# Layer 1's last couple in seven factor products, and layer 2's weights prepared in two thirds of the steps

## The chip, the core and the metric

The kernel runs on one core of a Trainium2 chip. TensorE (PE) multiplies 128x128 weight tiles with a moving tile of up to 512 columns into PSUM banks; VectorE (DVE) and ScalarE (ACT) do the elementwise work, each strictly in the order in which its instructions were issued; GpSimd (POOL) does one small operation per attention tile; SyncE (SP) issues the DMAs, also in order. The metric is the device time of one execution in microseconds. A difference of 0.2% (3.1 us) is about what a measurement can tell from no change.

## The reference

```python
kv = einsum('bhsd,bhse->bhde', k, v);  out = einsum('bhsd,bhde->bhse', q, kv)      # linear attention
x = out / sqrt(mean(out*out, -1) + 1e-6) * g_norm                                   # per head of 64
x = x.transpose(0, 2, 1, 3).reshape(4608, 512)
h = x @ w_in1;  x = (h * sigmoid(1.702 * h)) @ w_out1                               # layer 1, d_ff 2048
h = x @ w_in2;  r = maximum(h, 0);  y = (s * r * r + b) @ w_out2                    # layer 2
```

All in float32. The weights come as float64 words and are turned into float32 on the chip; every product is made of three matmuls on a high and a low part of its operands.

## The kernel before, in words

The 4608 tokens are nine blocks of 512. **Head.** The first 48 steps (FIRST to `N1`, here S0 to S47) compute layer 1 for blocks 0, 1 and 2, one step for one 128-row slice f of the hidden layer: 12 matmuls into one `h` bank (`mm1`), Gelu on ACT (`act_g`), a split into high and low parts, 12 matmuls of the second product (`mm2`) two steps later. Blocks 0 and 1 run first, S32 to S47 are block 2 alone, with a single `h` bank (`h0`). Beside them, layer 1's weights are converted (`to_f32`), split and stored, the sums of its first product's factors are prepared (`prep_first`), and attention tiles are computed.

**Pairs.** What is left is computed in couples of two blocks, by a scheme that needs 7 block products where plain blocking needs 8. Layer 1 has three couples (blocks 3 to 8), layer 2 four couples and one single block. A couple is worked off in 8 pairs of slices, a pair in 7 ticks; a tick is one `product` of 6 matmuls (of the first product, `x @ w_in`), what `after` does with it, and one unit of the second product. I count ticks from the first pair: couple 1 is T0 to T55, couple 2 T56 to T111, couple 3 T112 to T167, layer 2 from T168.

Second product, before: in layer 1 every pair has 8 `units` of 6 matmuls each, 4 into a passing bank (name `z`), whose result DVE adds to a sum in SBUF, and 4 into banks that stay (`sum`). The passing bank is `h1` alone up to pair 12 and alternates between `h1` and `a1` from pair 13 (`FREE_A`); `a1` serves the attention tiles meanwhile. With one bank the next z unit cannot begin before DVE's addition of the last is done. In layer 2 the second product too is made in seven factor products: two pairs form a quad, which has 14 `quad_unit`s of 6 matmuls (name `m` for a passing, `msum` for a staying bank), preceded by additions (`factor_add`) and splits (`factor_hi`, `factor_lo`) on ACT and DVE, and followed by `combine` at the couple's end. The quads use `wraw0`, `wraw1`, `wst0`, `wst1` for their raw tiles, the same places that the preparation of layer 2's weights uses.

**Beside the pairs.** Attention tiles for the coming couple are placed by hand (`tiles_in`): in pairs 1, 2, 4, 5 and 9 to 12, at tick 0 and tick 3 of the pair `att_u` (PE), `att_sq` (ACT) and `att_r` (DVE, `ms<-xn`, then POOL), two ticks later `att_norm` (DVE, `xn<-u,r`), and after the product of the third tick `att_turn` (PE, `xtp<-ident,xn`). Everything else is a `Task`, stepped in `background` at a tick's end when its due time has come or the metered load of ACT and DVE is below a limit. Two tasks prepare layer 2's weights: `convert2` (float64 words to float32, 32 slices, 2 ACT and 5 DVE operations each) and `prepare2` (sums `wc`, splits through staging tiles `wst`, stores). Before, they start at about T6 and their due times run to T165.

Of the kernel before, what the change touches and what calls it, by code (L numbers as in the profile page):

```python
# [44 lines left out]
ROOM = 500.0  # L45

# [6 lines left out]
def tile_attn_moe_moe2(  # L53
# [101 lines left out]
    def to_f32(which, ph, f):  # L155
# [5 lines left out]
        w = rot("wf", 3, (P, DM), U32)  # L161
# [58 lines left out]
    def spaced():  # L220
        while couples_on and now[0] < stored[0] + 2:
            yield 1
        stored[0] = now[0]

    def parts_hl(dst, src, n):

        yield
        yield from spaced()
        t = rot("wst", 2, (P, 2, 2, KP), F32R)[:, 0:n]
# [3 lines left out]
        if isinstance(dst, list):  # L233
            for x, part in enumerate(dst):
                move(part, t[:, x])
        else:
            move(dst, t)
# [29 lines left out]

    wt_dram = {}

    def prep_out(p):  # L270

        wa, wb = (w_raw.pop((1, 1, f)) for f in (2 * p, 2 * p + 1))
        if p == 0:
            wt_dram.update({x: dp.tile([P, 8, 2, 2, KP], F32, name=f"wt{x}") for x in range(KF // 4)})
        a, b = (x.rearrange("p (h e) -> p h e", h=2) for x in (wa, wb))
        d = wt_dram[p // 2][:, :, p % 2]
        c = new("wc", (P, 4, KP))
        tt = vector.tensor_tensor
# [235 lines left out]
    def fac_sums(s):  # L514
# [10 lines left out]
        if s > first2:  # L525
# [7 lines left out]
    def split_x(s, i):  # L533

        lay, m, _ = couples[s]
        if i == 6 and s > first2:
# [18 lines left out]
    made2 = [0, 0]  # L555

    def convert2():

        for m, (which, f) in enumerate(order2):
            made2[0] = m  # L560
            while m >= made2[1] + 3:
                yield 1
            for n, _ in enumerate(to_f32(which, 1, f)):
                yield 1 if n == 0 else 0
            if m + 2 < len(order2):
                load_w(order2[m + 2][0], 1, order2[m + 2][1])
        made2[0] = len(order2)

    def prepare2():

        for m, (which, f) in enumerate(order2):
# [4 lines left out]
            yield from (prep_in, prep_out)[which](f // 2)  # L576
            made2[1] = m + 1
# [69 lines left out]
    P2 = first2 * (KF // 2)  # L647
    place_of = {}
# [53 lines left out]

    def width(P_):
# [3 lines left out]
    def c_new(P_, e):  # L707

        if layer(P_):
            q_, m = (P_ - P2) // 2, width(P_)  # L710
# [33 lines left out]
    def g_hi(P_, e):  # L744

        if layer(P_):
            return
# [12 lines left out]
    def g_lo(P_, e):  # L760
        if layer(P_):
# [46 lines left out]
    def units(P_):  # L808
# [48 lines left out]
    FREE_A = 13  # L857
    BY = 2
    FACTORS = 7
# [3 lines left out]
    quads = [(s_, x) for s_ in range(first2, LAST) for x in range(KF // 2 // BY)]  # L863
    t_t, f_t, mid_t, m_ps, m_sb = {}, {}, {}, {}, {}
    t_next = [0]

    def load_t():
# [3 lines left out]
        if n < len(quads) * FACTORS:  # L871
            q_, k_ = divmod(n, FACTORS)
            t = t_t[q_, k_] = new(f"wo{n % T_RING}", (P, 2, 2, KP), F32R)
            move(t, wt_dram[quads[q_][1]][:, k_])
        elif n < len(quads) * FACTORS + KF - 2:
            load_last(n - len(quads) * FACTORS, f"wo{n % T_RING}")

    def load_last(f, tag):
        t = t_t["last", f] = new(tag, (P, 2, 2, KP), F32R)
        move(t, wt_dram[f // 4][:, (slice(0, 8, 7), slice(5, 7))[f % 2], f // 2 % 2])  # L880
# [130 lines left out]
    def combine(s):  # L1011
# [4 lines left out]
        def send(k_, t, right, h):  # L1016
            row, col = js[t] * BT, (2 * right + h) * P
            turns["z"] = turns.get("z", -1) + 1
            z = new(("tr0", "kv0", "kv1")[turns["z"] % 3] if last else ("tr0", "ev0", "g1")[turns["z"] % 3], name="turned")
# [63 lines left out]
    def load_wo2():  # L1083
# [4 lines left out]
        if n < first2 * KF:  # L1088
# [86 lines left out]
    for x, slot in ((0, 2), (0, 2), (0, 5), (0, 5), (1, 5)):  # L1175
        at((P2 + x, slot), "load", load_t)
# [35 lines left out]
    for p in range(KF // 2):  # L1212
        todo.setdefault(10 + 4 * p, []).append((prep_first, p))
# [9 lines left out]
    for m in range(2):  # L1223
        at(len(steps) - 3 + m, "raw", load_w, 0, 1, m)
# [16 lines left out]
    def plan():  # L1241
# [3 lines left out]
        for s_ in range(len(couples)):  # L1245
            n0 = n * s_
            need = []
            if s_:
                if couples[s_][0]:
                    need = [Task(y_get(s_), n0 - n + 6, n0 - n + 7)]  # L1250
                if s_ < LAST:
                    need = [Task(fac_sums(s_), n0 - (14 if s_ <= first2 else 35), n0 - 9, need)]
            for i in range(7 if s_ < LAST else 2):
                if (s_, i) in split_early:
                    continue
                more = [split[s_, 1]] if (i == 6 and s_ <= first2 and (s_, 1) in split) else []
                split[s_, i] = Task(split_x(s_, i), max(0, n0 - 7 + i + 1), max(0, n0 + i - (4 if i < 6 else 5)), need + more)
            if first2 <= s_ < LAST:
# [17 lines left out]
    with tc.manual_schedule():  # L1276
# [204 lines left out]

        split_early = [(0, i) for i in range(4)]
# [6 lines left out]
        for n in range(FIRST, N1):  # L1489
            conv = to_f32(*convs.pop(n)) if n in convs else iter(())  # L1490
            start(n)
            run(n, "splith")
# [9 lines left out]
            run(n, "pe")  # L1502
            next(conv, None)
# [7 lines left out]
            next(conv, None)  # L1511
            y_out(n - 2, 2)
# [7 lines left out]
            make()  # L1520
            make()
            make()
            if n == N1 - 5:
                load_half(0)
# [38 lines left out]
        for P_, (s_, p) in enumerate(pairs):  # L1563
            lay, m, js = couples[s_]
            for i in range(7):
# [4 lines left out]
                at_q = ((P_ - P2) // BY, 7 * (P_ % BY) + i)  # L1570
                after(P_, i)
                if lay:
# [16 lines left out]
                elif i == 2 and layer(P_ - 1) == 0:  # L1589
                    running.append(units(P_ - 1))  # L1590
                for _ in range({6: 2}.get(i, 1) if P_ < P2 else 1 if P_ == P2 or i % 2 == 0 else 0):
# [3 lines left out]
                if lay:  # L1595
# [3 lines left out]
                background(tick, slot, SLACK, ROOM if lay and P_ > P2 + 1 else 9999.0)  # L1599
# [87 lines left out]
```

## Time and profile before

| | |
|---|---|
| three runs | 1569.70, 1569.93 (median), 1570.78 us |
| profiled execution | 1572.51 us, its span 1570.7 us |
| PE busy | 1550.3 us, 99% of the span |
| DVE, ACT busy | 1021.4 us (65%), 936.1 us (60%) |
| DMA | 372.56 MB, mean 237 GB/s |

The columns of the rows further below: a line of the timeline has the start from the span's begin, the duration, engine, line, operation, output and inputs by the program's names, shapes, count, and in brackets the idle time of the engine before it and what ended it. Matmuls of 512 columns show 0.39 us each but start 0.23 us apart: they overlap, so PE's pace is read from the starts. The page and the views name DVE's and ACT's work by one line (L89), that of a helper.

### The profile page before, as it was taken

To read this page: it belongs to the slowest core of one execution; us is meant where nothing else is said; L and a number is where in the kernel's file an instruction comes from. 1 tells how busy PE (TensorE), PEld (TensorE's weight loads), DVE (VectorE), ACT (ScalarE), POOL (GpSimd) and SP (SyncE) were. 2 spreads that over 40 slices of the span, in tenths; PEclk is the share of its full clock that TensorE was granted. 3 is DMA by queue.
4 is the path that set the end of the run, shared out by engine and by line. 5 is a ranking of instruction groups with operands and counts; after the bars stand their busy time and mean duration, and the time that the engine had idled before them with its cause. 6 is when DMAs were issued, how large, how long until landed. Compare 5 with 4: busy or idle time off the path is not lost.

```text
span 1570.7 us, 20568 instructions
## 1 busy us (share of the span) xinstructions
PE 1550.3 (99%) x7536; PEld 1272.0 (81%) x7536; DVE 1021.4 (65%) x1510; ACT 936.1 (60%) x1520; POOL 69.3 (4%) x49
## 2 busy tenths in 40 slices
PE   8999999999999999999999999999999999999999
PEld 7788887878887788888888888788878887888887
DVE  6877733357567666786877366877687768756631
ACT  4766643455455545465445876876687667766652
POOL 3000111201000011000000000000000000000000
PEclk9999999999999999999999999999999999999999
DMA  8679878557876976679885856587568756876574
GB/s 278 192 259 317 287 238 271 202 200 242 276 235 213 319 242 224 229 280 372 330 314 191 285 193 190 191 245 246 188 200 234 238 192 201 224 231 195 189 215 121
DMA packets 185910, 372.56 MB, mean 237 GB/s; under 512 B 79698, under 2 KB 88146, under 8 KB 178642
## 3 DMA queue, kind: packets, MB, share of 16 engines
q1 hardware_dynamic: 185666, 371.12, 71.8%
q8 instruction: 60, 0.98, 0.3%
q14 instruction: 40, 0.33, 0.1%
q10 hardware_dynamic: 144, 0.13, 0.0%
HBM read 289.41 MB, written 81.79 MB: 236 GB/s over the span
## 4 chain that ended last, share of the span: by engine, by line
PE 89%; DVE 5%; ACT 3%; DMA 2%; issue 1%; SPq 0%; POOL 0%; ACTq 0%; DVEq 0%; POOLq 0%
PE A L696 6%; PE A L697 6%; PE A L698 6%; PE m L994 4%; PE m L993 4%; PE m L992 4%; PE D L696 3%; PE D L697 3%; PE D L698 3%; PE z L830 3%; PE sum L830 3%; PE sum L832 3%; PE sum L831 3%; PE z L832 3%; PE z L831 3%; PE acc L624 3%
## 5 line engine op out<-in xcount | busy, mean ns | idle before, releaser
L89 ACT ACTIVATE gh<-gh 128x512 f32<-128x512 f32 x72 | 45.4, 632 | 145.0 <-DVE gh L89 144.8
L994 PE MATMUL m<-fac,wo 128*128 128x512 f32 x320 | 125.2, 391 | 1.1 <-DVE fac L89 1.1
L992 PE MATMUL m<-fac,wo 128*128 128x512 f32 x320 | 125.8, 393 | 0.0
L993 PE MATMUL m<-fac,wo 128*128 128x512 f32 x320 | 125.7, 393 | 0.0
L696 PE MATMUL A<-wi,xl 128*128 128x512 f32 x296 | 116.7, 394 | 1.9 <-ACT wst L89 0.7
L698 PE MATMUL A<-wi,xl 128*128 128x512 f32 x296 | 115.3, 390 | 0.0
L697 PE MATMUL A<-wi,xl 128*128 128x512 f32 x296 | 115.3, 389 | 0.0
L89 DVE TENSOR_TENSOR madd<-m,madd 128x512 f32<-128x512 f32 x122 | 83.8, 687 | 45.8 <-PE m L994 45.7
L89 ACT ACTIVATE wraw<-wraw 128x512 uint32<-128x512 uint32 (+1 forms) x128 | 82.8, 647 | 48.9 <-DVE wraw L89 48.3
L425 POOL TENSOR_TENSOR r<-ms,mhalf 128x8 f32<-128x8 f32 x36 | 65.6, 1825 | 545.7 <-DVE ms L89 545.6
L89 DVE TENSOR_TENSOR fac<-s,fac 128x1024 fp32r<-128x1024 f32 x64 | 77.9, 1218 | 5.5 <-ACT fac L89 5.4
L89 ACT ACTIVATE g<-h 128x512 f32<-128x512 f32 x52 | 31.0, 597 | 79.7 <-PE h L598 70.1
L596 PE MATMUL h<-xh,wi 128*128 128x512 f32 x192 | 76.5, 398 | 1.2 <-ACT g L89 1.2
L830 PE MATMUL z<-wo,wo 128*128 128x512 f32 x192 | 76.1, 396 | 1.2 <-DVE g L89 0.7
L624 PE MATMUL acc<-gh,wo 128*128 128x512 f32 x192 | 76.7, 399 | 0.0
L625 PE MATMUL acc<-gh,wo 128*128 128x512 f32 x192 | 75.0, 391 | 0.8 <-DVE wo L89 0.8
L626 PE MATMUL acc<-gl,wo 128*128 128x512 f32 x192 | 74.9, 390 | 0.0
L598 PE MATMUL h<-xl,wi 128*128 128x512 f32 x192 | 74.9, 390 | 0.0
L832 PE MATMUL z<-wo,wo 128*128 128x512 f32 x192 | 74.8, 390 | 0.0
L831 PE MATMUL z<-wo,wo 128*128 128x512 f32 x192 | 74.8, 389 | 0.0
L597 PE MATMUL h<-xh,wi 128*128 128x512 f32 x192 | 74.8, 389 | 0.0
L994 PEld LDWEIGHTS m<-fac,wo 128*128 128x128 f32 x320 | 59.9, 187 | 16.2 <-DVE fac L89 2.3
(265 smaller groups left out, 4221.4 us busy)
## 6 DMA issues: line engine op xcount, KB each, us to landing
wo<-wt SPq DMA_DIRECT2D x127, 512.0 KB, 4.0
wo<-wo SPq DMA_DIRECT2D x80, 512.0 KB, 5.1
xl<-wi SPq DMA_DIRECT2D x37, 1024.0 KB, 6.4
xl<-wi SPq DMA_DIRECT2D x37, 768.0 KB, 5.6
wi<-wst SPq DMA_DIRECT2D x40, 512.0 KB, 4.4
xh<-wi SPq DMA_DIRECT2D x19, 1024.0 KB, 6.4
wraw<-in_w_in SPq DMA_DIRECT2D x32, 512.0 KB, 4.1
wraw<-in_w_out SPq DMA_DIRECT2D x32, 512.0 KB, 4.7
```

What stands on the lines that cost most here:

```text
L89: return fn(*args, **kw)
L596: nc.tensor.matmul(o, wh[:, cs], xh[:, c, :], start=(c == 0), stop=False)
L624: nc.tensor.matmul(o, wh[:, ds_], gh, start=(f == lo), stop=False)
L696: nc.tensor.matmul(o, wh, xh, start=(c == 0 and not more), stop=False, skip_group_check=more)
L697: nc.tensor.matmul(o, wl, xh, start=False, stop=False, skip_group_check=more)
L698: nc.tensor.matmul(o, wh, xl, start=False, stop=(c == 1), skip_group_check=more)
L830: nc.tensor.matmul(o, wh[:, cs], gh, start=begins, stop=False)
L831: nc.tensor.matmul(o, wl[:, cs], gh, start=False, stop=False)
L832: nc.tensor.matmul(o, wh[:, cs], gl, start=False, stop=ends)
L992: nc.tensor.matmul(o, w[:, y, 0, hs], hi[:, y, :], start=begins, stop=False)
L993: nc.tensor.matmul(o, w[:, y, 1, hs], hi[:, y, :], start=False, stop=False)
L994: nc.tensor.matmul(o, w[:, y, 0, hs], lo[:, y, :], start=False, stop=ends)
```

## The change

1. Couple 3 of layer 1 gets the quad scheme (`quads` begin at `firstq = first2 - 1`, pair `PQ` = 16). Its second product takes 84 matmuls for two pairs in place of 96; with 4 quads that is 336 in place of 384, so 48 matmuls fewer in all (the built programs have 6384 and 6336 matmuls of 512 columns). Its factors are prepared in the head by a new function `prep_first_out` (steps S33 to S45): for each of 8 pairs of slices two additions (`f5`), four subtractions (`wc`), two splits with their stores. Three of the seven factors are read back as two loads of 256 KB from the stored layer 1 weights.
2. Layer 2's weights have to be done before the quads of couple 3 begin. `convert2` starts in the head (two steps of it in each of S41 to S47), and both tasks get due times from a table `rate` by pairs of ticks: the work ends by T102. The limit on metered DVE work of a tick (`ROOM`) is 1300 in place of 9999 in layer 1's pairs.
3. Around it: a third staging place (`f5`, when it is free) and a wait of 3 ticks between uses of one; a store is issued at the next tick's `background` rather than at once; a fourth `wf` buffer (in `tr0`'s place); a slice is converted 3 ticks or more after its load was issued; `prep_first` comes in steps 10 to 30 in place of 10 to 38; two passing banks for z also in pairs 5, 6 and 12 (`FREE_A` 12).

```diff
-PLACES = ( ... xn0 xn1 wf0 tr0 ...
+PLACES = ( ... xn0 xn1 wf0 wf3 ...
+REUSE = 3
+F5_TAKEN = ((-99, 3), (41, 59), (97, 999))
...
-    def spaced():
-        while couples_on and now[0] < stored[0] + 2:
+    used = {"wst0": -99, "wst1": -99, "f5": -99}
+    def staging():
+        if not couples_on:
+            turns["wst"] = turns.get("wst", -1) + 1
+            places = ("wst0", "xh1", "xl1") if 33 <= now[0] < len(steps) - 5 else ("wst0", "wst1")
+            return new(places[turns["wst"] % len(places)], (P, 2, 2, KP), F32R, "wst")
+        while True:
+            free = [x for x in used if now[0] - used[x] >= REUSE and (x != "f5" or not any(lo <= now[0] <= hi for lo, hi in F5_TAKEN))]
+            if free and now[0] > stored[0]:
+                x = min(free, key=used.get)
+                used[x] = stored[0] = now[0]
+                return new(x, (P, 2, 2, KP), F32R, "wst")
             yield 1
...
+    def prep_first_out(p):
+        if p % 2 == 0:
+            wt_dram[0, p // 2] = dp.tile([P, FACTORS, 2, 2, KP], F32, name=f"wt0_{p // 2}")
+        d = wt_dram[0, p // 2][:, :, p % 2]
+        ab = new("f5", (P, 2, 2, KP))
+        for x in range(2):
+            parts = [part.rearrange("p (h e) -> p h e", h=2) for part in w_out[0, 2 * p + x]]
+            vector.tensor_tensor(out=ab[:, x], in0=parts[0].bitcast(F32), in1=parts[1].bitcast(F32), op=ALU.add)
+        yield
+        c = new("wc", (P, 4, KP))
+        yield from out_sums(ab[:, 0], ab[:, 1], c)
+        yield from parts_hl(d[:, 1:3], c[:, 0:2], 2)
+        yield from parts_hl(d[:, 3:5], c[:, 2:4], 2)
...
-            while m >= made2[1] + 3:
+            while m >= made2[1] + 4 or (couples_on and now[0] < loaded.get(m, -9) + 3):
                 yield 1
...
-                o = bank(("h1", "a1")[turns["m"] % 2 if P_ >= FREE_A else 0], "z")
+                o = bank(("h1", "a1")[turns["m"] % 2 if P_ >= FREE_A or P_ in (5, 6) else 0], "z")
...
-    FREE_A = 13
+    FREE_A = 12
...
-    quads = [(s_, x) for s_ in range(first2, LAST) for x in range(KF // 2 // BY)]
+    quads = [(s_, x) for s_ in range(firstq, LAST) for x in range(KF // 2 // BY)]
...
     for p in range(KF // 2):
-        todo.setdefault(10 + 4 * p, []).append((prep_first, p))
+        todo.setdefault((10, 14, 18, 21, 24, 26, 28, 30)[p], []).append((prep_first, p))
+    for p in range(KF // 2):
+        todo.setdefault(33 + 7 * p // 4, []).append((prep_first_out, p))
...
-        Task(convert2(), 7, lambda: 14 + made2[0] * 4.6)
-        Task(prepare2(), 5, lambda: 18 + made2[1] * 4.6)
+        Task(converting, 6, lambda: pace((steps2[0] - 15) / 145) - 1)
+        Task(prepare2(), 7, lambda: pace(steps2[1] / 144) + 1)
+    rate = [1.0] * 2 + [0.9] * 2 + [1.4] + [0.9] * 2 + [1.5, 1.2] + [0.9] * 5 + [1.6] * 2 + [1.2]
+    paces = [0.0]
+    for t in range(7, 102):
+        paces.append(paces[-1] + (0.4 if 52 <= t < 62 else rate[t // 7 + 1]))
...
-                background(tick, slot, SLACK, ROOM if lay and P_ > P2 + 1 else 9999.0)
+                background(tick, slot, SLACK, ROOM if P_ > PQ + 1 else 1300.0)
```

How the change moves instructions is shown at three places. The first is DVE's order in T7 to T9, the first attention tile of the pairs (`ms<-xn` begins it, `xn<-u,r` ends it; `gh<-B` is the work on the tick's product; `wf` is `convert2`, `wc` `prepare2`). Before:

```order
L89 TENSOR_REDUCE ms<-xn 128x8
L89 TENSOR_SCALAR ms<-ms 128x8
L89 TENSOR_TENSOR gh_3386<-B,gh_3386 128x512
L89 TENSOR_SCALAR wf<-wf 128x512 x2
L89 SCALAR_TENSOR_TENSOR wf<-wraw,wf 128x512
L89 ISA wf<-wraw,wf 128x1024
L89 TENSOR_TENSOR xn<-u,r 128x512
```

After:

```order
L91 TENSOR_REDUCE ms<-xn 128x8
L91 TENSOR_SCALAR ms<-ms 128x8
L91 TENSOR_SCALAR wf<-wf 128x512 x2
L91 SCALAR_TENSOR_TENSOR wf<-wraw,wf 128x512
L91 ISA wf<-wraw,wf 128x1024
L91 TENSOR_TENSOR gh_3548<-B,gh_3548 128x512
L91 TENSOR_TENSOR wc<-wf 128x256
L91 TENSOR_TENSOR wc<-wc,wf 128x256
L91 TENSOR_TENSOR wc<-wf 128x256
L91 TENSOR_TENSOR wc<-wf,wc 128x256
L91 TENSOR_TENSOR xn<-u,r 128x512
```

A conversion now stands ahead of the product's addition, and four `wc` subtractions ahead of the norm.

The second is DVE's order in T63 to T65, the same three steps of an attention tile in pair 9. Before:

```order
L89 TENSOR_REDUCE ms<-xn 128x8
L89 TENSOR_SCALAR ms<-ms 128x8
L89 TENSOR_SCALAR wf<-wf 128x512 x2
L89 SCALAR_TENSOR_TENSOR wf<-wraw,wf 128x512
L89 ISA wf<-wraw,wf 128x1024
L89 TENSOR_TENSOR gh_4994<-B,gh_4994 128x512
L89 TENSOR_TENSOR wc<-wf 128x256
L89 TENSOR_TENSOR wc<-wf,wc 128x256
L89 TENSOR_TENSOR wc<-wf 128x256
L89 TENSOR_TENSOR wc<-wf,wc 128x256
L89 TENSOR_SCALAR wf<-wf 128x512 x2
L89 TENSOR_TENSOR xn<-u,r 128x512
```

After:

```order
L91 TENSOR_REDUCE ms<-xn 128x8
L91 TENSOR_SCALAR ms<-ms 128x8
L91 TENSOR_SCALAR wf<-wf 128x512 x2
L91 SCALAR_TENSOR_TENSOR wf<-wraw,wf 128x512
L91 ISA wf<-wraw,wf 128x1024
L91 TENSOR_TENSOR gh_5280<-B,gh_5280 128x512
L91 TENSOR_TENSOR wst<-wc,wst 128x2x256
L91 TENSOR_TENSOR xn<-u,r 128x512
```

Here six preparation operations have gone from ahead of the norm, and one split has come.

The third is ACT's order in S37 and S38 of the head (`kvbd<-kvps` and `xn<-u` are attention, `g<-h` is the Gelu that frees the one `h` bank). Before:

```order
L89 COPY kvbd_74<-kvps 64x4x64 x2
L89 ACTIVATE xn<-u 128x512
L89 ACTIVATE g<-h 128x512
L89 CAST gh<-g 128x512
L89 ACTIVATE f_2495<-xtp,g_67 128x2x128
```

After:

```order
L91 COPY kvbd_74<-kvps 64x4x64 x2
L91 ACTIVATE xn<-u 128x512
L91 CAST wst<-wc 128x2x256
L91 ACTIVATE g<-h 128x512
L91 CAST gh<-g 128x512
L91 ACTIVATE f_2552<-xtp,g_67 128x2x128
```

One split of `prep_first_out` now stands between the attention square and the Gelu.

## Rows read from the trace of the kernel before

**Rows 1.** The page: span, and busy time of PE and DVE.
```profile
span 1570.7 us, 20568 instructions
PE 1550.3 (99%) x7536; PEld 1272.0 (81%) x7536; DVE 1021.4 (65%) x1510; ACT 936.1 (60%) x1520; POOL 69.3 (4%) x49
```

**Rows 2.** Busy time by stretch: T7-27, T28-55, T84-104, both halves of couple 3, a layer-2 couple.
```profile
core 0: us, PE busy (x) PEld busy (x) DVE busy (x) ACT busy (x) POOL busy (x), PEclk, DMA share, GB/s
...
344.80:414.10 69.30, 68.75 (x394) 55.77 (x395) 45.28 (x82) 35.97 (x69) 7.16 (x4) 1.00 0.77 261
414.10:503.00 88.90, 87.96 (x409) 72.43 (x408) 61.78 (x105) 46.14 (x83) 7.46 (x4) 1.00 0.71 239
...
598.10:663.60 65.50, 64.97 (x296) 53.06 (x295) 45.45 (x81) 31.61 (x58) 3.64 (x2) 1.00 0.68 237
684.00:765.60 81.60, 81.60 (x362) 67.59 (x361) 61.20 (x101) 43.88 (x78) 0.00 (x0) 1.00 0.91 335
765.60:847.20 81.60, 81.60 (x362) 67.59 (x361) 67.37 (x104) 39.28 (x69) 0.00 (x0) 1.00 0.77 281
1035.20:1189.50 154.30, 153.95 (x673) 125.91 (x672) 112.17 (x134) 112.83 (x167) 0.00 (x0) 1.00 0.72 218
```

**Rows 3.** PE's waits over the whole span: total us, times, longest us.
```profile
PE h L596 <- ACT g L89: 1.2, 1, 1.2
PE m L994 <- DVE fac L89: 1.1, 3, 0.4
...
PE z L830 <- DVE g L89: 0.7, 2, 0.6
...
PE z L830 <- DVE gl L89: 0.4, 1, 0.4
```

**Rows 4.** PE's timeline: T10, T20, a z unit of T47, and T66.
```profile
352.13 0.39 PE L696 MATMUL D<-wi,xl 128*128 128x512 f32 x1
...
353.49 0.60 PE L435 MATMUL xtp<-ident,xn 128*128 128x128 f32 x4
...
386.67 0.60 PE L435 MATMUL xtp<-ident,xn 128*128 128x128 f32 x4
...
475.19 0.39 PE L698 MATMUL D<-wi,xl 128*128 128x512 f32 x1
475.96 0.50 PE L830 MATMUL z<-wo,wo 128*128 128x512 f32 x1 [0.37 <-DVE gl L89]
...
538.42 0.63 PE L435 MATMUL xtp<-ident,xn 128*128 128x128 f32 x4 [0.57 <-DVE xn L89]
```

**Rows 5.** DVE's timeline: the attention tiles of T7, T17 and T63.
```profile
348.83 0.69 DVE L89 TENSOR_REDUCE ms<-xn 128x8 f32<-128x512 f32 x1 [1.63 <-ACT xn L89]
...
349.64 0.68 DVE L89 TENSOR_TENSOR gh<-B,gh 128x512 f32<-128x512 f32 x1
...
352.59 0.68 DVE L89 TENSOR_TENSOR xn<-u,r 128x512 f32<-128x512 f32 x1
...
380.67 0.69 DVE L89 TENSOR_REDUCE ms<-xn 128x8 f32<-128x512 f32 x1 [0.83 <-ACT xn L89]
...
531.68 0.69 DVE L89 TENSOR_REDUCE ms<-xn 128x8 f32<-128x512 f32 x1 [3.93 <-ACT xn L89]
...
535.33 0.41 DVE L89 TENSOR_TENSOR wc<-wf 128x256 f32<-128x256 f32 x1
...
536.79 0.88 DVE L89 TENSOR_SCALAR wf<-wf 128x512 f32<-128x512 f32 x2
537.59 0.68 DVE L89 TENSOR_TENSOR xn<-u,r 128x512 f32<-128x512 f32 x1
538.19 0.68 DVE L89 COPY g<-z 128x512 f32<-128x512 f32 x1
```

**Rows 6.** ACT's timeline: S38 of the head, and T7.
```profile
267.47 0.60 ACT L89 ACTIVATE xn<-u 128x512 f32<-128x512 f32 x1 [8.96 <-PE xtp L435]
...
348.20 0.60 ACT L89 ACTIVATE xn<-u 128x512 f32<-128x512 f32 x1 [0.64 <-PE u L407]
```

More of the change, by code (lines that the diff above doesn't have):

```diff
@@ L232, in parts_hl, with store @@
         vector.tensor_tensor(out=t[:, :, 1, :], in0=src, in1=t[:, :, 0, :].bitcast(F32), op=ALU.subtract)
[L233 to L237, printed above, removed]
+        stores.append((dst, t))
+        if not couples_on and not 33 <= now[0] < len(steps) - 5:
+            store()
+    stores = []
+    def store():
+        while stores:
+            dst, t = stores.pop(0)
+            if isinstance(dst, list):
+                for x, part in enumerate(dst):
+                    move(part, t[:, x])
+            else:
+                move(dst, t)
     def sums_of(a, b, c):
@@ L566, in convert2 @@
                 load_w(order2[m + 2][0], 1, order2[m + 2][1])
+                loaded[m + 2] = now[0] if couples_on else -9
         made2[0] = len(order2)
@@ L575, in prepare2 @@
                 continue
-            yield from (prep_in, prep_out)[which](f // 2)
-            made2[1] = m + 1
+            for wait in (prep_in, prep_out)[which](f // 2):
+                steps2[1] += wait != 1 or stored[0] == now[0]
+                yield wait
     steps = [(j, f, lo, hi) for j, lo, hi in PARTS for f in range(lo, hi)]
@@ L707, in c_new @@
     def c_new(P_, e):
[L709 to L710 removed]
+        if quad(P_):
+            q_, m = (P_ - PQ) // 2, width(P_)
             if (q_, e) not in raws:
@@ L744, in g_hi @@
     def g_hi(P_, e):
-        if layer(P_):
+        if quad(P_):
             return
@@ L760, in g_lo @@
     def g_lo(P_, e):
-        if layer(P_):
+        if quad(P_):
             return
@@ L1223, in tile_attn_moe_moe2 @@
     for m in range(2):
-        at(len(steps) - 3 + m, "raw", load_w, 0, 1, m)
+        at(len(steps) - 9 + m, "raw", load_w, 0, 1, m)
     tasks = []
@@ L1502, in tile_attn_moe_moe2 @@
             run(n, "pe")
+            for _ in range(0 if n < 21 else 1):
+                make()
             next(conv, None)
@@ L1511, in tile_attn_moe_moe2 @@
             next(conv, None)
+            for _ in range(0 if n < 21 else 1):
+                make()
             y_out(n - 2, 2)
@@ L1519, in tile_attn_moe_moe2 @@
             run(n, "load")
-            make()
-            make()
-            make()
+            for _ in range(3 if n < 21 else 2):
+                make()
+            if n >= N1 - 7:
+                for _ in range(2):
+                    next(converting)
             if n == N1 - 5:
+                store()
                 load_half(0)
@@ L1588, in tile_attn_moe_moe2 @@
                             y_out(N1 - 1, d)
-                elif i == 2 and layer(P_ - 1) == 0:
+                elif i == 2 and not quad(P_ - 1):
                     running.append(units(P_ - 1))
-                for _ in range({6: 2}.get(i, 1) if P_ < P2 else 1 if P_ == P2 or i % 2 == 0 else 0):
+                for _ in range({6: 2}.get(i, 1) if P_ < PQ else 1 if P_ == PQ or i % 2 == 0 else 0):
                     while running and next(running[0], StopIteration) is StopIteration:
```

80 lines of the change are left out of this document (54 added, 26 removed), and 2 rows, old and new, of the table PLACES.

## Prediction

> **What bounds the kernel now.** I read the page first: PE is busy 1550.3 of 1570.7 us [rows 1]. With PE at 99%, only two things can change the time: how many matmuls there are, and the idle time on PE. Second, the busy time by stretch [rows 2]: in couple 3 (the rows 684.00 and 765.60) PE is busy for all of its 163.2 us, so there a matmul that is taken away is time that is taken away, unless something else becomes late. The same rows show how near the others are: DVE 67.37 of 81.60 us (0.83) in the second half, DMA at 0.91 and 335 GB/s in the first, and still no idle PE. Third, PE's waits [rows 3, 4]: they are short and few, and most are on DVE (norm of an attention tile, addition of a z unit). So DVE's order beside the pairs is where a price would be paid. What lies outside the span is 1572.51 - 1570.7 = 1.8 us and stays. The profiled execution is 2.6 us above the median of the three runs, so I make the sum as a difference and take it from the median.
>
> **Part 1, the quads of couple 3: -8.9 us.** Couple 3 has 8 pairs of 42 + 48 matmuls, 720, and takes 163.2 us, 0.2267 us for one [rows 2]. A couple of layer 2 has 8 x 42 + 336 = 672 and takes 154.3 us (the row 1035.20 of [rows 2]), 0.2296 us for one, its own short waits within. Couple 3 becomes such a couple, so 163.2 - 154.3 = 8.9 us go. At couple 3's own pace it would be 48 x 0.2267 = 10.9 us, and I keep this as the other end. I take 8.9, since the row is a couple that is done in just this way. The step from units to quads, with its thin ticks, moves from couple 4 to couple 3 and keeps its price. The new ACT and DVE work of the quads falls into T112 to T180, and preparation work leaves the same ticks: DVE has 112.17 of 154.3 us in a layer-2 couple (0.73) against 128.6 of 163.2 (0.79) in couple 3 now [rows 2]. Gelu in place of ReLU and squares is less for ACT. I cost this at nothing; the wait for the factors that every quad couple pays once, 0.4 us (m in [rows 3]), is within 154.3.
>
> **Part 2, the same preparation in fewer ticks.** I counted DVE's operations tick by tick in both orders and priced each by the distance from its start to the next start: 0.60 us for 512 elements (537.59 to 538.19), four `wc` operations 1.46 (535.33 to 536.79), a pair of `wf` 0.80 (536.79 to 537.59), a whole conversion 352.59 - 349.64 - 0.60 = 2.35, the reduce with its small partner 349.64 - 348.83 = 0.81 [rows 5]. By this T28 to T55 get 12 us more DVE work, T84 to T102 10 us, T7 to T27 11 us, T56 to T83 8 us. With what they have now [rows 2] the first becomes 73.8 of 88.9 us (0.83), T7 to T27 56 of 69.3 (0.81), and T84 to T104 55.5 of 65.5 (0.85). That is what the second half of couple 3 shows without any idle PE, but there two banks take z in turn and no attention tile runs. So I go through the places where PE waits for DVE within a tick or two.
>
> *z units on one bank.* Pairs 5, 6 and 12 get a second bank. The rows z <- DVE of [rows 3] are three waits, 1.1 us; two of them are in T47 and T53, units of pairs 5 and 6, the other is a unit of pair 12. Each also costs in restarting: at 475.96 the start is 0.77 us after 475.19 and not 0.23, so 0.54 for a shown 0.37, and the next starts late too; I take 0.27 more for one. They go: -(1.1 + 3 x 0.27) = -1.9 us. In the other pairs one bank remains. There the ticks with z units get at most 11.8 us of DVE work in four ticks of 2.9 us, and T30 to T33 carry 11.5 us before and show no wait, so I cost this at nothing; the rival below takes the other end.
>
> *Norms that are now early.* At T63 the reduce starts at 531.68, the transposition was due at 538.42 - 0.57 = 537.85, so DVE has 6.2 us from the reduce to the end of the norm [rows 4, 5]. Before, twelve operations stood in there; after, a split in place of `wc` x4 and `wf` x2: 2.26 - 0.60 = 1.7 us less, more than the 0.57 it was late. The like holds at T84. With the other of these waits about 0.3 and the restarts, -1.4 us.
>
> *Norms that are now late.* T7 is the worst. ACT has two more operations of a conversion ahead of the square, 1.1 us, of which its idle 0.64 [rows 6] takes a part: the reduce starts about 0.45 later, 349.3. From there to the norm it was 352.59 - 348.83 = 3.76 us, and with four `wc` it is 5.2; the norm starts at 354.5 and ends at 355.2, while PE transposed at 353.49 [rows 4, 5]: 1.7 us late, 1.9 with the restart. Within this the product of T10 (due 352.13) waits, since `gh<-B` now stands behind the conversion and must free its bank. At T14 and T35 the operations from reduce to norm add up to 6.4 us against 6.2: 0.2 and the restart, 0.45 each, 0.9 us. At T31, T66, T73, T80 and T87 they add up to 6.1 to 6.4 us where the window of such a tile is 6.0 (T17: 380.67 to 386.67 [rows 4, 5]): 0.4 each, 2.0 us; between 0, if the window is a little wider, and 3.
>
> *Head.* `prep_first_out` adds about 30 us of DVE work to S33 to S47, where a step lasts near 6 us and DVE has 2 to 4 us of work; the heaviest three steps, S43 to S45, get 19.7 us in some 18. What they delay is needed a step and a half later, so nothing. ACT is the tighter one: at S38 it sits 8.96 us on the attention square, and the Gelu behind it holds the only `h` bank; PE waits 1.2 us there [rows 3, 6]. One split now stands between, 0.53 us: +0.5. For other places of this kind, and staging tiles that share `wst1` with the evictions, I take another 0.5, with 0 and 2 as ends.
>
> *Stores and loads.* The preparation's transfers are pressed into fewer ticks; by the bytes of the DMAs in the order, T28 to T55 go from 236 to 306 GB/s. The row at 335 GB/s has PE fully busy [rows 2]. Nothing. That stores are issued a tick later, when their data is there, frees SP's queue for the loads behind them.
>
> **Sum.** -8.9 - 1.9 - 1.4 + 1.9 + 0.9 + 2.0 + 0.5 + 0.5 = -6.4 us. From the median 1569.9 this gives 1563.5 us.
>
> **Rivals.** *Fewer waits than counted.* The norms that are 0.2 us late by a sum of a dozen prices may be in time, and couple 3 may run at 0.2267 us a matmul: -8.9 to -10.9, -1.9, -1.4, +1.9, +0.5, so 1558 to 1560 us. For it: PE's idle time now is a few us in all; against: seven norms would all have to come in time.
>
> *Every DVE operation counts with its full duration.* A row has 0.69 us where the next start is 0.60 later; if operations with waits between do not overlap that much, each of about six of them ahead of a norm costs 0.09 more, 0.5 at each of eight places and at T7, some 4.5 us: 1563.5 + 4.5 = 1568 us. Against it: at T63 my prices give 6.6 us and the rows give 6.6. [...]
>
> *DVE becomes the bound on one bank (the other side).* In pairs 0 to 4 and 7 to 11 there are 40 z units on one bank. PE has 6 matmuls of the next product, 1.36 us, between two of them, and the addition takes 0.69: if DVE comes to it more than about 0.6 us late, PE stops. It decides from where DVE's work between two z units exceeds 3.3 us. If half of them lose the 0.54 us of T47's row, that is 20 x 0.54 = 10.8 us more, 1574 us. For it: DVE goes to 0.81 to 0.85 there; against: T30 to T33.
>
> *The loads come late.* A raw slice has three ticks, 8.7 us, from issue to conversion; if DMA at 306 GB/s makes these late, ACT stands, and with it Gelu and the bank copies. 32 slices at 0.1 us are 3 us: 1566.5 us. Against it: the row at 335 GB/s.
>
> **How the numbers follow.** My forecast, 1561 to 1566.5 us, has 0.55; fewer waits 0.17; full durations 0.08; one bank 0.08; loads 0.12. Faster by over 0.2% (3.1 us, what a measurement tells from no change) is below 1566.8: 0.55 + 0.17 + half of the loads, 0.78. Within: full durations, the other half, a little of one bank, 0.15. Slower 0.07. The range leaves out the lower end of fewer waits and one bank: 1559.5 to 1567.5 us.
>
> **What would show it.** T112 to T223 shorter by about 9 us, with PE busy throughout; no z waits at T47 and T53; xtp waits at T10 of 1 to 2 us and short ones at T17, T38 and T69; the one wait of h near 1.7 us. I am wrong if z units wait in many ticks of pairs 1 to 5 and 8 to 12, if ACT waits for `wraw`, or if PE idles in the last steps of the head.

## The result: 0.8% slower

The changed kernel takes 1583.84 us, median of six runs (1582.64 to 1584.71), the kernel before 1570.82 us beside it (1569.70 to 1571.81): ratio 1.0083, interval 1.0070 to 1.0096. The forecast was 1563.5 us, in a range of 1559.5 to 1567.5. Profiled, its span is 1582.9 us against 1570.7 us [rows 1].

The stretches of the two traces, from the first product of S0, T0, T56, T112, T168 and T224 (us):

| | start | head | couple 1 | couple 2 | couple 3 | layer 2, first couple | rest |
|---|---|---|---|---|---|---|---|
| before | 27.0 | 297.4 | 178.7 | 181.0 | 163.2 | 148.7 | 574.8 |
| after | 25.2 | 299.3 | 196.8 | 182.9 | 149.8 | 153.8 | 575.2 |
| difference | -1.8 | +1.9 | +18.1 | +1.9 | -13.4 | +5.1 | +0.4 |

(The start is left out below: it differs by as much between kernels that are the same up to there, 27.0 us in the kernel before and 25.3 in its variant g1 of the experiments.) So the gain of the quads came: couple 3 and the couple after it, 311.9 us before, take 303.6. By stretch, columns as in [rows 2], first the changed kernel from T112:

```profile
704.20:854.00 149.80, 148.25 (x650) 121.22 (x648) 97.60 (x109) 68.28 (x99) 0.00 (x0) 1.00 0.73 254
854.00:1007.80 153.80, 153.80 (x673) 126.12 (x674) 107.10 (x125) 108.84 (x161) 0.00 (x0) 1.00 0.67 219
```

then the kernel before from its T112:

```profile
684.10:847.30 163.20, 163.20 (x722) 135.18 (x721) 128.58 (x204) 83.16 (x146) 0.00 (x0) 1.00 0.84 308
847.30:996.00 148.70, 148.01 (x650) 121.56 (x649) 84.77 (x96) 104.91 (x158) 0.00 (x0) 1.00 0.64 213
```

The loss is in T0 to T111, 20.0 us, nearly all in couple 1. PE's longest waits there, in the changed kernel (total us, times, longest):

```profile
PE u L453 <- ACT f L91: 4.7, 3, 3.0
PE D L750 <- ACT gh L91: 4.1, 2, 3.1
PE A L750 <- ACT ev L91: 2.1, 2, 1.4
PE xtp L481 <- DVE xn L91: 1.4, 4, 0.5
```

In the same ticks of the kernel before, PE's waits are 3.6 us in all, 1.9 on DVE and 1.7 on ACT. Now they are 15.5 us, 12.8 of them on ACT, and ACT itself waits for DMA. Its waits for stores of staging tiles in T0 to T111, after:

```profile
ACT wst L91 <- DMA wi<-wst: 14.3, 6, 5.1
ACT wst L91 <- DMA wt<-wst: 12.1, 4, 5.4
```

and all of that kind in the same ticks before:

```profile
ACT wst L89 <- DMA wi<-wst: 0.3, 1, 0.3
```

The largest case is T31, in the changed kernel. SP's queue (a row is the issue of a DMA), then ACT, then PE:

```profile
418.77 0.38 SPq L127 DMA_DIRECT2D wi<-wst  x1
419.27 0.36 SPq L127 DMA_DIRECT2D xl<-wi  x1
420.66 0.33 SPq L436 DMA_DIRECT2D q<-in_q  x1
421.10 0.80 SPq L127 DMA_DIRECT2D wi<-wst  x1
```
```profile
425.45 0.62 ACT L91 CAST wst<-wf 128x512 fp32r<-128x512 f32 x1 [4.18 <-DMA wi<-wst]
...
429.76 0.62 ACT L91 CAST wst<-wc 128x512 fp32r<-128x512 f32 x1 [2.04 <-DMA wi<-wst]
430.28 0.58 ACT L91 COPY gh<-A 128x512 f32<-128x512 f32 x1
...
431.75 0.85 ACT L91 ACTIVATE f<-xtp,g 128x256 f32<-128x256 f32 x2
```
```profile
429.31 0.40 PE L889 MATMUL z<-wo,wo 128*128 128x512 f32 x1
432.66 2.07 PE L453 MATMUL u<-kvbd,q 128*128 128x128 f32 x8 [2.95 <-ACT f L91]
434.38 0.77 PE L750 MATMUL A<-wi,xh 128*128 128x512 f32 x1
434.96 0.63 PE L751 MATMUL A<-wi,xh 128*128 128x512 f32 x1
435.38 0.63 PE L752 MATMUL A<-wi,xh 128*128 128x512 f32 x1
```

Read from the bottom: PE stands 2.95 us for `f`, the copy of a transposed attention tile, which ACT issues only at 431.75, since in front of it in ACT's order stand two splits (CAST wst). The first may write its place when the store issued at 418.77 has landed, 6.7 us later, the second when the one of 421.10 has, 8.7 us later. Behind the gap the matmuls start 0.42 us apart instead of 0.23: the granted clock fell. By 5 us stretches of the changed kernel:

```profile
425.00:430.00 5.00, 4.63 (x21) 3.16 (x20) 3.34 (x6) 2.52 (x5) 0.00 (x0) 1.00 1.00 411
430.00:435.00 5.00, 2.34 (x10) 2.25 (x11) 1.98 (x3) 2.84 (x7) 0.00 (x0) 0.71 1.00 396
435.00:440.00 5.00, 5.00 (x15) 3.92 (x14) 2.63 (x5) 2.64 (x5) 1.64 (x1) 0.61 0.85 274
```

T31 takes 4.4 us more than before, T32, at the lower clock, 2.1 more. The DMA engines are full (share 1.00 at 411 GB/s): the stores stand in a burst of loads. The same happens at T46, T48, T53 and T54, 7.5 us in all.

Why a split meets a store that has not landed can be counted in the order of the instructions. A split is in tick n, the subtraction in n+1 at the earliest; the store is issued with it before, at the next tick's `background` after. Before, three ticks or more lie between a store's issue and the next split into its place, in all cases; after, in 22 of 63 cases it is one tick, 3.2 us on the mean of couple 1 before (178.7 / 56; the expectations' 4.8 for one tick and 14 for three are too long). The time from issue to landing of the staging stores, min, median and max over some T20 to T57, before:

```profile
DMA to landing us min/median/max: 2.0/3.7/7.3
```

and after:

```profile
DMA to landing us min/median/max: 2.8/5.8/9.7
```

Over all of T0 to T111 the median is 3.3 us before and 4.7 after, and the longest 9.7 us in both. (Some of these stores are halves, of 256 KB.) So landings of this length are not new. Before, three ticks lie between, and ACT waits 0.3 us.

### The profile page after: what moved, and what is told of

Read it like the earlier page. It is cut to its first block, busy times and chain, and to the rows that moved or that the text cites. A ratio compares the mean times of both kernels' runs of the same rounds, so it can differ in the third digit from the quotient of the medians.

```text
span 1582.9 us, 20687 instructions
## 1 busy us (share of the span) xinstructions
PE 1548.1 (98%) x7488; PEld 1265.1 (80%) x7488; DVE 1088.1 (69%) x1600; ACT 957.8 (61%) x1539; POOL 67.7 (4%) x49
## 4 chain that ended last, share of the span: by engine, by line
PE 83%; DVE 7%; ACT 4%; DMA 4%; issue 1%; SPq 0%; POOL 0%; DVEq 0%; ACTq 0%; POOLq 0%
PE A L750 6%; PE A L752 6%; PE A L751 6%; PE m L1059 5%; PE m L1058 5%; PE m L1057 5%; PE D L750 3%; PE D L751 3%; PE D L752 3%; PE acc L676 2%; PE acc L677 2%; PE acc L678 2%; PE msum L1058 2%; PE msum L1057 2%; PE h L648 2%; PE h L650 2%
## 5 line engine op out<-in xcount | busy, mean ns | idle before, releaser
L1059 PE MATMUL m<-fac,wo 128*128 128x512 f32 x400 | 156.5, 391 | 1.0 <-DVE fac L91 1.0
L1057 PE MATMUL m<-fac,wo 128*128 128x512 f32 x400 | 157.2, 393 | 0.0
L1058 PE MATMUL m<-fac,wo 128*128 128x512 f32 x400 | 157.2, 393 | 0.0
L91 DVE TENSOR_TENSOR madd<-m,madd 128x512 f32<-128x512 f32 x152 | 104.2, 686 | 55.2 <-PE m L1059 55.0
L91 ACT ACTIVATE wraw<-wraw 128x512 f32<-128x512 f32 (+1 forms) x136 | 87.9, 646 | 66.6 <-DVE wraw L91 65.9
L91 DVE TENSOR_TENSOR fac<-s,fac 128x1024 fp32r<-128x1024 f32 x80 | 97.3, 1217 | 6.9 <-ACT fac L91 6.8
L1059 PEld LDWEIGHTS m<-fac,wo 128*128 128x128 f32 x400 | 74.9, 187 | 19.8 <-DVE fac L91 2.6
L1057 PEld LDWEIGHTS m<-fac,wo 128*128 128x128 f32 x400 | 75.1, 188 | 16.3
L1058 PEld LDWEIGHTS m<-fac,wo 128*128 128x128 f32 x400 | 75.1, 188 | 16.0
L91 ACT CAST fac<-s 128x1024 fp32r<-128x1024 f32 x80 | 83.6, 1045 | 0.0
L91 ACT ACTIVATE gh<-gh 128x512 f32<-128x512 f32 x48 | 30.2, 631 | 77.7 <-DVE gh L91 77.6
L91 ACT ACTIVATE wi<-wi 128x512 f32<-128x512 f32 x72 | 45.4, 630 | 52.5 <-DVE wi L91 51.5
```

Source lines behind the costliest of these rows:

```text
L91: return fn(*args, **kw)
L1057: nc.tensor.matmul(o, w[:, y, 0, hs], hi[:, y, :], start=begins, stop=False)
L1058: nc.tensor.matmul(o, w[:, y, 1, hs], hi[:, y, :], start=False, stop=False)
L1059: nc.tensor.matmul(o, w[:, y, 0, hs], lo[:, y, :], start=False, stop=ends)
```

## Experiments

Thirteen kernels, each timed beside the kernel before (ratios are to it). T0 to T111 took 359.7 us before; the last column but one is what it takes more.

| run | median us | ratio, interval | T0-T111 | ACT's waits for stores there |
|---|---|---|---|---|
| changed kernel | 1583.84 | 1.0083 (1.0070-1.0096) | +20.0 | 26.4 |
| e1_store_at_once | 1574.32 | 1.0021 (1.0012-1.0030) | +8.6 | 12.9 |
| e4_fourth_place | 1578.37 | 1.0048 (1.0033-1.0063) | +12.3 | 19.4 |
| e5_once_fourth_place | 1574.02 | 1.0016 (1.0006-1.0025) | +9.4 | 13.7 |
| e6_even_pace | 1578.21 | 1.0054 (1.0036-1.0073) | +12.5 | 27.7 |
| f1_three_ticks | 1572.12 | 1.0007 (0.9998-1.0015) | +6.7 | 2.0 |
| f2_three_ticks_even | 1571.82 | 1.0002 (0.9993-1.0010) | +5.5 | 0.4 |
| f3_three_ticks_slow42 | 1590.84 | 1.0126 (1.0110-1.0141) | +7.4 | 5.8 |
| f4_no_stores | 1573.01 | 1.0011 (1.0002-1.0020) | +7.7 | 0 |
| g1_before_one_place | 1618.73 | 1.0300 (1.0286-1.0314) | +25.0 | 75.7 |
| j1_three_ticks_beat | 1568.85 | 0.9982 (0.9973-0.9990) | +3.4 | 2.6 |
| j2_three_ticks_table | 1567.84 | 0.9979 (0.9970-0.9988) | +1.4 | 0 |
| j3_three_ticks_no_stores | 1571.96 | 1.0003 (0.9994-1.0012) | +6.5 | 0 |
| k1_no_split_cast | 1569.79 | 0.9989 (0.9980-0.9998) | +4.5 | 0 |

The theories: *staging* (the place of a staging tile is asked for again before its store has landed), *volume* or *bursts* (the DMA engines are full, whatever the places), *load* (too much work per tick), and later *order* and *ScalarE* (what stands in front of what on ACT). The expectations' 33.7 us of waits include 6 us of `ev` and 1.3 us of `wst` that lie in the head and stay in the run without layer 2's stores (4.6 and 1.5 us there); 26.4 us are those of T0 to T111.

**Is it the stores' place and time?**

```diff
-        if not couples_on and not 33 <= now[0] < len(steps) - 5:
+        if couples_on or not 33 <= now[0] < len(steps) - 5:
             store()
```

> The changed kernel with one edit: in the couples the store of a staging tile is issued right behind the subtraction that fills it, not at the next tick's background call. Staging theory: the loss of 13 us comes from ScalarE, which stands at a split (CAST wst) until the store that last left the same staging tile has landed (in the changed kernel's list of waits 14.3 + 13.4 + 6.0 us, 15 times), so that bank copies queued behind the split are late for TensorE. A store a tick (4.8 us) earlier lands a tick earlier; the three rows of waits fall from 33.7 us to under 12, the gaps of TensorE at 432, 486, 495 and 511 us shrink to under 1 us each, and the time falls by 5 to 10 us, to 1574 to 1579. Volume theory (99 MB instead of 85 MB pass in ticks T0 to T111, the DMA engines are full, a landing is late wherever the store stands in the queue): waits within a fifth of 33.7 us, time within 2 us of 1583.8. Load theory (VectorE and ScalarE have too much work per tick, since 145 preparation steps are done by T102): the same, no change.

1574.3 us, -9.5 against the changed kernel. The waits fell to 12.9 us, not under 12, T31 is only 0.5 us longer than before and T48 0.4. A tick more for the landing is worth half of the waits and 11.4 us of T0 to T111. T55, which lost 0.3 us, now loses 2.0.

```diff
+    staged = {"wst0": -99, "wst1": -99, "f5": -99, "f4": -99}
+    TAKEN = {"f5": F5_TAKEN, "f4": ((-99, 3), (39, 65), (97, 999))}
...
                 used[x] = stored[0] = now[0]
+                open_ = [y for y in staged if not any(lo <= now[0] <= hi for lo, hi in TAKEN.get(y, ()))]
+                x = min(open_, key=staged.get)
+                staged[x] = now[0]
```

> The changed kernel with the same order of every instruction; only the place that a staging tile gets is chosen among four instead of three where the tile f4 is free (T4 to T38 and T66 to T96), the one used longest ago. T41 to T59 keep their two places. Staging theory: the waits for stores in T4 to T38 and T66 to T96 vanish, with them the TensorE gap of 2.95 us at T31 and the lower clock behind it (T31 and T32 took 6.5 us more than before) and some of the 2.2 us at T73 and T80; the waits at T46 to T54 stay. Time 1575 to 1578. Volume theory and load theory: the same bytes and the same operations at the same places in each queue, so within 2 us of 1583.8.

1578.4 us. No instruction moved, no byte less, and the gap at T31 with its low clock is gone (6.5 us). T48 (1.6 us) and most of T53 stay, as they should; T46 and T54 lose their gaps too, while T55 (1.3 us) and T101 (1.1 us) get one, which staging had not said. T73 and T80 did not get shorter: they had been put down to stores wrongly.

> Both edits: stores issued at once, and the fourth staging place. Staging theory: nearly all of the 33.7 us of waits for stores go (under 5 us left), T31, T32 and T46 to T54 are within 1 us of their time before, and the time is 1568 to 1573, at or just below the kernel before. Volume theory and load theory: within 2 us of 1583.8.

1574.0 us, 1 us above what staging expected and no better than the first edit alone. The stretch with two places (T41 to T59) still has two ticks between store and split, and T55 and T56 lost 3.9 us there.

```diff
-        paces.append(paces[-1] + (0.4 if 52 <= t < 62 else rate[t // 7 + 1]))
+        paces.append(paces[-1] + 1.0)
```

> The changed kernel with an even pace of the preparation of layer 2's weights from T7 to T102, in place of the table that asks 1.4 to 1.5 of the mean at T21 to T27 and T42 to T48 and 0.4 at T52 to T61. Staging theory: the splits come no closer than 3 ticks on one place under either pace, so the waits move with the stores and the loads beside them; the sum of the three rows stays over 20 us and the time is within 5 us of 1583.8. Load theory: the peaks are what costs, T31, T46 to T54 lose their gaps, and the time falls to 1574 or below. Volume theory: the DMA share at 425 to 435 us falls from 1.00, and the time falls by 3 to 8 us.

1578.2 us, 5.6 below the changed kernel: within volume's range and 0.6 us outside staging's. The waits stayed (27.7 us), as staging said, but met PE less. Between staging and volume this run alone decides nothing.

**Three ticks, as before.** The first edit, `REUSE = 4`, and the fourth place asked for by the same rule:

```diff
-REUSE = 3
+REUSE = 4
-    used = {"wst0": -99, "wst1": -99, "f5": -99}
+    used = {"wst0": -99, "wst1": -99, "f5": -99, "f4": -99}
+    TAKEN = {"f5": F5_TAKEN, "f4": ((-99, 3), (39, 65), (97, 999))}
```

> The changed kernel with stores issued at once, four staging places (f4 in T4 to T38 and T66 to T96), and a place given again after four ticks instead of three, so that at least three ticks (14 us) lie between a store's issue and the next split into its place, as in the kernel before; in the changed kernel it is one tick in 22 of 63 cases. Staging theory: with the spacing of before, ScalarE's waits for stores fall to what they were before (5 us, 3 times), the gap of TensorE at T55 and T56 that was left with both edits (3.9 us) goes too, couple 3 starts 5 to 7 us later than before instead of 20 later, and the time is 1567 to 1571. Bursts theory (the waits come from loads and stores in flight together, at a DMA share of 1.00, so that a landing takes 8 to 9 us wherever the store is): some of the waits stay, time 1572 to 1576.

1572.1 us, the waits 2.0 us in T0 to T111, and T55 is as before. The DMA engines are as full as they were, but PE no longer stands. The 10 us around T31 in the changed kernel, then in this run:

```profile
425.00:435.00 10.00, 6.97 (x31) 5.40 (x31) 5.33 (x9) 5.35 (x11) 0.00 (x0) 0.85 1.00 404
425.00:435.00 10.00, 10.00 (x51) 8.42 (x50) 8.17 (x16) 5.63 (x12) 1.64 (x1) 1.00 1.02 412
```

The spacing takes back 11.7 us of the loss; staging's range was missed by 1 us, since new waits of PE came at T68 (a z unit, 1.2 us) and T76 (a norm, 0.95 us).

> As the run with three ticks, with an even pace from T7 to T102 in place of the table. Staging theory: waits for stores near 5 us here too, so the pace now shows its own worth: where the table puts less preparation beside attention work, an even pace makes norms and bank copies late. Time 1569 to 1576. Bursts theory: an even pace spreads the bytes, 1567 to 1571.

1571.8 us (the pace line of the even run on top): the table is worth nothing against an even pace here.

> As the run with three ticks, but with a pace of 0.6 in T42 to T61 in place of 1.5, 1.2 and 0.4, so that the stretch in which only two staging places exist has fewer splits, and T62 to T101 more. Staging theory: no waits for stores left; time 1567 to 1572, depending on what the more crowded T62 to T101 costs. Load theory (work per tick is what costs): T73, T80 and T87 get longer by 1 us each, 1572 to 1575.

1590.8 us, far outside every range. (Here the fourth place is chosen as in the second edit.) T0 to T111 is 7.4 us longer, no worse than its kin; the rest comes in couple 3. With the slow stretch the last splits and their stores slip to T113 to T117, where the quads of couple 3 take `wst0` and `wst1` for raw tiles. ACT, and SP's row of the store it waited for:

```profile
710.46 0.59 ACT L91 COPY wst<-A 128x512 f32<-128x512 f32 x1 [12.36 <-DMA wt<-wst]
```
```profile
703.91 0.38 SPq L127 DMA_DIRECT2D wt<-wst  x1
```

The split was finished at T115, at 702.1; its store was issued at 703.91, behind three loads, and ACT's copy of a bank of couple 3 waited for it until 710.46. T115 and T116 take 10.2 us more than before. It comes once more: ACT stands 6.8 us until 725.37, for a store issued at 720.21, and T118 and T119 take 7.5 us more than in the changed kernel. The same mechanism, twice. The changed kernel issues its last staging store at T110 (its table asks for T102), so its couple 3 is free of this.

**What do the stores cost in all?** Left out: layer 2's stores.

```diff
         while stores:
             dst, t = stores.pop(0)
+            if couples_on:
+                continue
...
```

> The changed kernel without the stores of layer 2's prepared weights (left out: those stores; layer 2's products read layer 1's prepared weights in their place, the same number of bytes). Nothing waits for a store then, and 28 MB of traffic are gone. Staging theory: this is the floor of what the stores cost; T31, T32 and T46 to T56 are as long as before or shorter, couple 3 starts 4 to 7 us later than before, time 1566 to 1570, equal to the run with three ticks within 2 us. Bursts theory: it is faster than the run with three ticks by over 3 us, since the traffic costs by itself. Load theory: still over 1578.

1573.0 us, within 1 us of three ticks, as staging said, but 3 us above its range: T55, T73 and T80 stay longer than before. It is 10.8 us below the changed kernel by the medians; by the two traces T0 to T111 is 20.0 - 7.7 = 12.3 us shorter. (The stores are 64 of 512 KB, 34 MB; the expectation said 28.) With three ticks, taking them out as well:

> The run with three ticks without the stores of layer 2's prepared weights (left out: those stores; layer 2's products read layer 1's prepared weights in their place), every other instruction in the same order. It shows what the stores still cost there. Staging theory with three ticks being enough: within 1.5 us of 1572.1. Bursts theory (28 MB of stores slow every other transfer): 1568 to 1570.

1571.96 against 1572.12 us: with the spacing right, 34 MB of stores cost nothing that a measurement can tell. Volume and bursts fall: a landing takes up to 9.7 us, but that costs only where somebody waits for it within that time.

**Does the spacing alone do it, in the kernel before?**

```diff
-        t = rot("wst", 2, (P, 2, 2, KP), F32R)[:, 0:n]
+        t = rot("wst", 1 if couples_on else 2, (P, 2, 2, KP), F32R)[:, 0:n]
```

> The kernel before with one edit: in the couples the staging tiles share one place instead of two. Its pace of preparation, its bytes and its deferral of nothing stay as they are; only the time from a store's issue to the next split into the same place goes from three ticks or more to one tick in 27 cases of 39. Spacing theory (one tick is too short for a landing of 3 to 4 us plus the issue, at any volume): ScalarE waits for stores in many places, over 40 us in all, and the kernel is slower by 10 to 40 us, 1581 to 1611. Bursts theory (the spacing hurts only where the changed kernel's higher volume stretches a landing to 8 us): under 10 us of waits more, 1570 to 1574.

1618.7 us, 47.5 us slower, more than the top of the range. ACT's waits in T0 to T111:

```profile
ACT wst L89 <- DMA wt<-wst: 42.7, 15, 5.6
ACT wst L89 <- DMA wi<-wst: 33.0, 13, 6.4
```

So the spacing needs no higher volume to cost. (Couple 3, into which this kernel's preparation reaches, takes 21 us more too.)

**What is left: 7.7 us in T0 to T111.** In the run without stores PE waits for ACT at T55, T66, T73 and T80. ACT at T55 and T56, where Gelu (`ev<-A`) is due:

```profile
502.58 0.63 ACT L91 ACTIVATE gh<-gh 128x512 f32<-128x512 f32 x1 [5.53 <-DVE gh L91]
503.12 0.60 ACT L91 CAST wst<-wf 128x512 fp32r<-128x512 f32 x1
503.63 1.04 ACT L91 CAST wi<-f 128x1024 fp32r<-128x1024 f32 x1
504.58 0.62 ACT L91 ACTIVATE gh<-gh 128x512 f32<-128x512 f32 x1
505.11 0.61 ACT L91 CAST wst<-wc 128x512 fp32r<-128x512 f32 x1
505.62 1.05 ACT L91 CAST wi<-f 128x1024 fp32r<-128x1024 f32 x1
506.56 0.65 ACT L91 ACTIVATE wf<-wraw 128x512 f32<-128x512 f32 x1
507.12 0.63 ACT L91 ACTIVATE wraw<-wraw 128x512 uint32<-128x512 uint32 x1
507.66 0.57 ACT L91 ACTIVATE ev<-A 128x512 f32<-128x512 f32 x1
```

Eight operations in a row without a pause, behind 5.53 us of standing for DVE's `gh`. To test it, the splits are taken from ACT (left out besides the stores: the splits' high parts):

```diff
-        scalar.copy(t[:, :, 0, :], src)
+        if couples_on:
+            clock["act"] += 95 + 512 * 0.83
+        else:
+            scalar.copy(t[:, :, 0, :], src)
...
```

> The run without stores, and without ScalarE's 64 splits (CAST wst) in the couples (left out: the stores and the high parts of layer 2's prepared weights; VectorE subtracts as before, from another operand). Every other instruction stands in the same order. ScalarE theory (what remains of the loss in T0 to T111 is in part ScalarE's preparation work standing ahead of Gelu and of the bank copy of an attention tile, at T55, T66, T73 and T80): each of these waits of TensorE shrinks by about the 0.5 us of a split, the one at T55 by more, and the time is 1569 to 1571, 2 to 4 us below the run without stores (1573.0). VectorE theory (the waits come from its order alone): the waits stay and the time is within 1 us of 1573.0.

1569.8 us, -3.2. PE at T55 and T66, without stores:

```profile
508.29 0.50 PE L752 MATMUL A<-wi,xl 128*128 128x512 f32 x1 [1.31 <-ACT ev L91]
...
546.34 1.16 PE L455 MATMUL u<-kvbd,q 128*128 128x128 f32 x8 [0.82 <-ACT f L91]
```

and without ACT's splits too:

```profile
509.36 0.50 PE L756 MATMUL A<-wi,xl 128*128 128x512 f32 x1 [0.28 <-ACT ev L91]
...
546.88 1.16 PE L459 MATMUL u<-kvbd,q 128*128 128x128 f32 x8 [0.29 <-ACT f L91]
```

T66, T73 and T80 are each 0.53 us shorter, one split, T55 1.02, two. So ACT's splits are 2.6 us of the loss in these ticks. T55, T73 and T80 remain 0.5 to 0.7 us longer than before, and at T55 ACT still stands for DVE.

**A pace that fits.** Three ticks, with another table. First, nearly even, but slow in the ticks with a reduce (the first and fourth of an attention pair):

```diff
+    rate = [1.0, 1.0, 1.3, 1.0, 1.1, 1.0, 1.0, 1.1, 1.0, 1.0, 1.0, 1.3, 1.5, 0.7, 1.0, 1.0, 1.0]
+    beat = [0.7, 1.2, 1.2, 0.3, 1.2, 1.2, 1.2]
+        paces.append(paces[-1] + rate[t // 7] * (beat[t % 7] if t // 7 in (1, 2, 4, 5, 9, 10, 11, 12) else 1.0))
```

> The run with three ticks, with another pace: nearly even over T7 to T101, but 0.7 and 0.3 in the ticks of a pair's first and fourth product, where an attention tile's reduce stands and its norm follows, and 1.2 in the other five, for the pairs that carry attention work. Order theory (with the stores out of the way, what is left of the loss in T0 to T111 is preparation work standing ahead of norms on VectorE and of bank copies on ScalarE): the waits at T68, T76 and T83 (3.2 us) go, couple 3 starts 3 to 4 us later than before instead of 6 to 7, and the time is 1567 to 1570. Load theory (the sum of work per tick counts, not its place): within 1 us of 1572.

1568.9 us. T55, T73, T76 and T80 are as before; T68, which order had expected to go, is still 1.2 us longer, and T97 is 1.5. Second, with `rate = [1, 0.9, 0.9, 1.4, 0.9, 0.9, 1.4, 1.0, 0.7, 0.4, 0.9, 0.8, 0.9, 1.7, 1.6, 1.2, 1]` and `beat = [1.0, 0.6, 1.0, 1.0, 1.0, 1.0, 1.0]`:

> The run with three ticks, with the changed kernel's table shifted a little: 0.4 for the pair of T63 to T69, 1.4 and 1.0 at T42 to T55, 1.7 at T91 to T97, and 0.6 in each attention pair's second product. Order theory: 1567 to 1570 as for the other pace, since the waits at T68 and T76 go here too. Load theory: the more crowded T91 to T102 costs what T63 to T69 gains, 1571 to 1573.

1567.8 us: 0.21% faster than the kernel before, about what can be told from no change, and 1.0% faster than the changed one, the best of this study. T55, T73 and T80 are as before within 0.1 us, T66 is 0.9 us shorter. PE's longest waits in T0 to T111 there:

```profile
PE xtp L482 <- DVE xn L91: 1.2, 4, 0.5
PE D L751 <- DVE gh L91: 0.9, 1, 0.9
PE A L751 <- ACT ev L91: 0.7, 1, 0.7
```

The order theory holds against the load theory: in the first of the two the same work is done by T107, at other ticks. In the second the last splits slip into couple 3, as in the run with the slow stretch: at T115 ACT waits 3.3 us for a store, and couple 3 takes 1.6 us more than in the changed kernel. So this gain is not all that the scheme can give.

## Why the prediction was wrong

The sum said -6.4 us, the traces say +14.0 without the start (+1.9, +20.0, -8.3, +0.4). The difference of 20.4 us, by the steps:

- **Quads of couple 3: -8.9 predicted, -8.3 measured.** Right, thin ticks included: they moved from layer 2's first couple (+5.1) into couple 3.
- **"Stores and loads. Nothing."** This is the step that failed: 12.3 us by the traces, 10.8 by the medians (changed kernel against the run without stores). It took the mean rate, 306 GB/s, and a row with 335 GB/s and no idle PE. The rate was right: with three ticks T28 to T55 run at 314 GB/s with PE busy for 88.4 of 89.1 us. But in the row with 335 GB/s ACT does wait for stores, 2.2 and 0.7 us, with three ticks between and PE not held up; a rate says nothing of the landing of one transfer behind a burst. "Issued a tick later ... frees SP's queue" saw the queue and not the place that the store keeps taken: with `REUSE = 3` one of the three ticks was left. It was all in the order: 22 times one tick. The price of a landing was in the trace of before too (median 3.3, up to 9.7 us).
- **The rival "the loads come late"** had the way it went, DMA late, ACT standing, Gelu and bank copies behind it. But it named the raw slices, which had been given three ticks; ACT's waits for `wraw` with `wf` behind them are 6.3 us against 5.2 before, all of them in the head. It gave 3 us.
- **Only DVE was counted tick by tick.** "DVE's order beside the pairs is where a price would be paid" left ACT out in T0 to T111. Without stores, T55 is 1.6, T73 1.0 and T80 1.2 us longer, and T66 0.2 longer where 0.9 less was to be had; the splits' share of it is 2.6 us in those four ticks and 3.2 in all. At T66, T73 and T80 a tile is turned and another begins; what was late there is ACT's copy of the turned tile (and at T55 Gelu), which the prediction had not counted.
- **Norms that are early: -1.4 predicted.** T87 gave -0.6; T63's norm did come in time, and the gain went to that ACT copy.
- **Norms that are late: +4.8 predicted.** T9 and T10 +1.9, as predicted (the wait for D is 0.87 us, for xtp 0.50); T17 and T38 +1.4 where 0.9 was expected. The five tiles that begin at T31, T66, T73, T80 and T87 are turned at T34, T69, T76, T83 and T90, which take 0.8 us more together and not 2.0, nearer to the rival of fewer waits.
- **Second bank for z: -1.9 predicted, -2.4 measured** at T47, T53, T95 and T96 in the run without stores (in the changed kernel a wait for a store covers T53). Two ticks with one bank (T40, T89) lost 0.5 each. The rival of DVE as the bound on one bank did not come.
- **Head: +1.0 predicted, +1.9 measured.** S38 is 0.5 us longer and its `h` wait 1.7 us, as predicted; S26 to S29 add 1.4, where `prep_first` comes sooner and PE waits 2.3 us for DVE's `wo`. The prediction did not count these steps.

Some 2 us of the 7.7 in T0 to T111 is in small differences of other ticks, whose cause stays open.

None of the three signs of being wrong came up (z waits in many ticks, more waits for `wraw`, idle PE at the end of the head): none of them was about stores.

## What to carry to other kernels

For a buffer that is filled, stored and filled again, lay the order out in time: from the store's issue (not the allocation, and not the last write) to the next write, against the longest landing seen in a burst (here 9.7 us, near three ticks), not against a mean rate. A counter that starts at the allocation loses every later deferral from this margin. Then count every in-order engine in front of the bottleneck, not the busiest alone: ACT at 61% held PE up, through what stood ahead of a copy.

## What was not expected of the hardware

Stores of 512 KB, all alike, took from 2.8 to 9.7 us to land in the changed kernel between T20 and T57. The DMA share was 0.48 during the shortest landing and 1.02 during the longest. The longest took 3.5 times as long as the shortest, so one figure for a landing does not tell when a place is free in a loaded queue.

The granted clock: with the 2.95 us of idle PE at T31 it was 0.71 and then 0.61 in stretches of 5 us, and 0.50 in the stretch from 433 to 438 us; matmuls started 0.42 us apart behind the gap. T31 and T32 take 6.5 us more than before, 3.6 more than the idle time. Around the 1.31 us at T55 of the run without stores it stayed at 1.00.
